# Sigmoid attention with a gated feed-forward: scores of whole key groups as three float32r products on two 64-row tiles, and six and six feed-forward tiles

## The chip, the cores and the metric

The kernel runs on one core of one Trainium2 chip. The metric is the time of one execution on the device in microseconds (us), the median of the runs shown; less is better. The profile is that of one more execution, with the hardware profiler on.

## The reference

Eight sequences of 448 tokens, 12 heads of 64 dimensions, everything in float32. Attention has a sigmoid in place of the softmax, so that no row sums are needed; its output is the input of a gated feed-forward layer of 768 to 1536 to 768.

```python
scores = scale * np.matmul(q, k.transpose(0, 1, 3, 2)) - np.log(S)
attn = 1.0 / (1.0 + np.exp(-scores))
x = np.matmul(attn, v)            # then (8*448) tokens x 768
...
gate = 1.0 / (1.0 + np.exp(-(x @ w_gate)))
val = x @ w_val
return (gate * val @ w_out).astype(np.float32)
```

The weights arrive as float64 words, which the kernel turns into a float32r part and a rest (hi and lo) by integer operations.

## The kernel before

**Attention** (lines 193 to 307). The work goes by quads of four heads: 24 quads, `m` from 0 to 23, each with the heads of two pairs, `p` 0 and 1. A quad's 448 keys of the two pairs make seven groups `g`: 0 to 2 are three groups of 128 keys of pair 0, 4 to 6 those of pair 1, and group 3 holds the last 64 keys of both pairs. One group is one beat, 168 beats in all. In each beat `scores` makes four products (the 128 keys in two halves `u`, the two heads of the pair in two halves of the partitions `h`), each 64 rows by 64 columns of the array with 448 queries streaming. The operands are float32, and TensorE runs every such product as two instructions, so that a line of four products is eight matmuls. Then comes one sigmoid on ScalarE (L221), and, two beats later (`LAG`), `values`: again four products of 64 by 64, in float32, which add up in four PSUM banks `av`.

**Beside it**, in the same loop: every second beat or so, VectorE does half of a conversion of a piece of weights (`Words.first`, L99 to L102, and `Words.second` with `finish_lo`, L112 to L118; GpSimd casts the hi part, L141). The first `J1` of twelve feed-forward tiles are converted here, 12 half steps a tile, spread over the first 156 beats (`BESIDE`). When a pair of heads is done, ScalarE copies one accumulator (L245), VectorE adds the other (L252), and the result goes to DRAM. `load_qk(m + 1)` is issued at the end of beat `g == 1`, `load_v(m + 1)` at `g == 3`. All DMAs go through SyncE's queue in the order of the program, and each engine works strictly in the order in which the loop is written.

**Feed-forward** (lines 310 to 387). For each of seven token tiles, `ff_in` makes gate and value of each feed-forward tile `j`, 36 matmuls of 128 by 128 by 512 in float32r (each product as lo·hi, hi·lo and hi·hi), and `ff_out` contracts with `w_out`, three products a tile likewise. Part one does this for the tiles `0..J1-1`, writes partial sums to DRAM and converts the other tiles (`late`) on VectorE beside it (`convert_ahead`, two half steps a call of `ff_in`); part two does the late tiles and adds the partial sums.

Of the kernel before, what the change touches and what calls it, by code (L numbers as in the profile page):

```python
# [9 lines left out]
F32R = mybir.dt.float32r  # L10
# [3 lines left out]
ALU = mybir.AluOpType  # L14
# [3 lines left out]
P = 128  # L18
HP = P // 2

F64_ZERO = 2.0 ** -15

J1 = 7

TB = 512

# [8 lines left out]
def sigmoid_attention_glu_kernel(ctx: ExitStack, tc: tile.TileContext, qk, v, wg, wv, wo, out):  # L35
# [10 lines left out]
    nc = tc.nc  # L46
    B, NQ = qk.shape[0], qk.shape[1]
    D = v.shape[-1]
    T = out.shape[-1]
    S = T // B  # L50
# [5 lines left out]
    scale = 1.0 / math.sqrt(D)  # L56
    late = list(range(J1, NJ))

# [17 lines left out]
    def chunks(j, t):  # L76
        w = (wg, wv, wo)[t]
        return [w[j][:, c * CW:(c + 1) * CW] for c in range(2)]
# [52 lines left out]
    def convert_tiles(words, js):  # L131

        for j in js:
            gv, wt = gv_tile(j, j), wo_tile(j, j)
            for to in (gv[:, 0], gv[:, 1], wt):
                for c in range(2):
                    cs = slice(c * CW, (c + 1) * CW)
                    words.first()
                    yield
                    hi, a, e = words.second()  # L140
                    nc.gpsimd.tensor_copy(to[:, 0, cs], hi)  # L141
                    finish_lo(to[:, 1, cs], a, e)
                    yield
# [27 lines left out]
    def load_x(t):  # L171
        for c in range(KT):
            xr[c] = xpool.tile([P, TB], F32, tag=f"xr{c}", name="xr")
            nc.sync.dma_start(out=xr[c], in_=x_dram[t][c])

    def split_x(cs=range(KT), cast=nc.scalar.copy):
        for c in cs:
            xh[c] = xpool.tile([P, TB], F32R, tag=f"xh{c}", name="xh")
            xl[c] = xpool.tile([P, TB], F32R, tag=f"xl{c}", name="xl")
            cast(xh[c], xr[c])  # L180
            nc.vector.tensor_tensor(out=xl[c], in0=xr[c], in1=xh[c], op=ALU.subtract)  # L181

    def store_x(b, c, x):

        at = b * S
        while at < (b + 1) * S:
            t, o = divmod(at, TB)
            n = min(TB - o, (b + 1) * S - at)
            nc.sync.dma_start(out=x_dram[t][c][:, o:o + n], in_=x[:, at - b * S:at - b * S + n])
            at += n  # L190


    halves = (slice(0, HP), slice(HP, P))
    with tc.manual_schedule(), tc.tile_pool(name="att", bufs=2) as att, tc.tile_pool(name="sc", bufs=2, space=PSUM) as scp, \
            tc.tile_pool(name="av", bufs=1, space=PSUM) as avp:
        loads, avs, pending, adds, stores = {}, {}, [], [], []

        def load_qk(m):

            if m < B * NQ:  # L200
                loads[m] = [att.tile([P, 2, 2 * S], F32, tag="qk", name="qk")]
                nc.sync.dma_start(out=loads[m][0], in_=qk[m // NQ, m % NQ])

        def load_v(m):
            if m < B * NQ:
                loads[m].append(att.tile([P, 7, 2, D], F32, tag="v", name="v"))
                nc.sync.dma_start(out=loads[m][1], in_=v[m // NQ, m % NQ])

        def scores(m, g):


            qkt = loads[m][0]
            sc = scp.tile([P, 2, 512], F32, tag="sc", name="sc")
            for h in range(2):
                for u in range(2):
                    p = u if g == 3 else g // 4
                    k0 = S + (3 * P if g == 3 else g % 4 * P + u * HP)
                    nc.tensor.matmul(sc[halves[u], h, :S], lhsT=qkt[halves[h], p, k0:k0 + HP], rhs=qkt[halves[h], p, :S],  # L218
                                     start=True, stop=True)
            a = att.tile([P, 2, S], F32, tag="a", name="a", bufs=3)  # L220
            nc.scalar.activation(a, sc[:, :, :S], AF.Sigmoid, bias=bias, scale=scale)  # L221
            return a

        def values(m, g, a):

            vt = loads[m][1]
            for u in range(2):
                p = u if g == 3 else g // 4
                key = (2 * m + p, u)
                start = key not in avs  # L230
                if start:
                    avs[key] = avp.tile([P, 512], F32, tag=f"av{p}{u}", name="av")
                last = (3 if u == 0 else 2) if p == 0 else 6
                for h in range(2):
                    nc.tensor.matmul(avs[key][halves[h], :S], lhsT=vt[halves[u], g, h], rhs=a[halves[u], h],  # L235
                                     start=start, stop=g == last)
            if g == 3:
                finish(2 * m)
            if g == 6:
                finish(2 * m + 1)  # L240

        def finish(n):
            b, c = divmod(n, 2 * NQ)
            x = att.tile([P, S], F32, tag="x", name="x")
            nc.scalar.copy(x, avs.pop((n, 0))[:, :S])  # L245
            adds.append((x, avs.pop((n, 1))[:, :S]))
            stores.append((beat + 2, b, c, x))

        def finish_adds():
            while adds:  # L250
                x, other = adds.pop()
                nc.vector.tensor_tensor(out=x, in0=other, in1=x, op=ALU.add)  # L252

        def finish_stores():
            while stores and stores[0][0] <= beat:
                store_x(*stores.pop(0)[1:])

        def load_first():

            loads[0] = [att.tile([P, 2, 2 * S], F32, tag="qk", name="qk")]  # L260
            for p, cs in ((0, slice(0, S + P)), (0, slice(S + P, 2 * S))):
                nc.sync.dma_start(out=loads[0][0][:, p, cs], in_=qk[0, 0][:, p, cs])
            load_v(0)
            nc.sync.dma_start(out=loads[0][0][:, 1], in_=qk[0, 0][:, 1])

        def warm_up(n):

            for _ in range(n):
                sc = scp.tile([P, 2, 512], F32, tag="sc", name="sc")
                for h in range(2):  # L270
                    for u in range(2):
                        nc.tensor.matmul(sc[halves[u], h, :S], lhsT=zeros[halves[h], :HP], rhs=zeros[halves[h], :S],  # L272
                                         start=True, stop=True)

        load_first()
        warm_up(2)
        words = Words(att, [c for j in range(J1) for t in (0, 1, 2) for c in chunks(j, t)], AHEAD)
        weights, n_weights, done = convert_tiles(words, range(J1)), 2 * 6 * J1, 0

        first_x = 2 * NQ + 2  # L280
        beat = 0
        for m in range(B * NQ):
            for g in range(7):
                pending.append((m, g, scores(m, g)))
                if len(pending) > LAG:
                    values(*pending.pop(0))
                finish_stores()
                if g == 1:
                    load_qk(m + 1)
                if g == LAG + 1:  # L290
                    load_v(m + 1)
                beat += 1
                while done < n_weights and done * BESIDE < beat * n_weights:
                    next(weights)
                    done += 1
                finish_adds()
                if m == first_x and g == 0:
                    load_x(0)
                if m == first_x + 1 and g < KT:
                    split_x([g], nc.gpsimd.tensor_copy)  # L300
        while pending:
            values(*pending.pop(0))
            finish_adds()
        beat += 2
        finish_stores()
        for _ in weights:
            pass


    with tc.manual_schedule(), tc.tile_pool(name="ff", bufs=2, reuse_waits="tile") as ff, \  # L310
# [52 lines left out]
        for part_two in (False, True):  # L363
            js = late if part_two else list(range(J1))
            for t in range(NT):
# [58 lines left out]
```

## Time and profile before

| | us |
|---|---|
| median of 3 runs | 1293.71 |
| lowest and highest | 1293.63, 1294.17 |
| the profiled execution, its own time | 1294.82 |
| its span, first to last instruction | 1292.7 |

The span is the time between the first and the last instruction that the profiler shows; about 2.1 us lie around it. The profiled execution was 1.1 us longer than the median.

A profile is read here by these views: the page's summary (busy time of each engine, the clock that TensorE was granted), the chain of work that ended last, the groups of instructions by line (count, busy time, mean length of one in ns, idle time before them), the timeline (start, length, engine, line, and in brackets the idle time before and what ended it), and windows (busy time of every engine in a stretch, with the number of instructions). PE is TensorE's matmul, PEld its weight load, DVE is VectorE, ACT ScalarE, POOL GpSimd, SP SyncE. The length of a matmul in the profile includes the way through the array, so that lengths overlap; the pace is read from the starts.

### The profile page before, as it was taken

To read this page: it belongs to the slowest core of one execution; us is meant where nothing else is said; L and a number is where in the kernel's file an instruction comes from. 1 tells how busy PE (TensorE), PEld (TensorE's weight loads), DVE (VectorE), ACT (ScalarE), POOL (GpSimd) and SP (SyncE) were. 2 spreads that over 40 slices of the span, in tenths; PEclk is the share of its full clock that TensorE was granted. 3 is DMA by queue.
4 is the path that set the end of the run, shared out by engine and by line. 5 is a ranking of instruction groups with operands and counts; after the bars stand their busy time and mean duration, and the time that the engine had idled before them with its cause. 6 is when DMAs were issued, how large, how long until landed. Compare 5 with 4: busy or idle time off the path is not lost.

```text
span 1292.7 us, 17701 instructions
## 1 busy us (share of the span) xinstructions
PE 1286.5 (100%) x7240; PEld 975.5 (75%) x7240; DVE 464.5 (36%) x920; ACT 358.5 (28%) x505; POOL 37.4 (3%) x52
## 2 busy tenths in 40 slices
PE   9999999999999999999999999999999999999998
PEld 4444444488888888888888888888888888888887
DVE  6778776445155252461310111202231213131312
ACT  6777777712112112121121121212020201111110
POOL 1112111000000000000000000000000000000000
PEclk9999999999999999999999999999999999999999
DMA  7777777343332332432002015241404131212202
GB/s 284 248 252 268 258 244 238 130 142 98 116 98 86 110 98 78 133 99 106 25 25 74 1 42 203 106 166 63 147 2 146 33 115 49 98 66 82 74 25 81
DMA packets 70784, 152.14 MB, mean 118 GB/s; under 512 B 9392, under 2 KB 26416, under 8 KB 70704
## 3 DMA queue, kind: packets, MB, share of 16 engines
q1 hardware_dynamic: 70704, 151.03, 34.6%
q8 instruction: 56, 0.92, 0.3%
q14 instruction: 24, 0.20, 0.0%
HBM read 106.17 MB, written 44.83 MB: 117 GB/s over the span
## 4 chain that ended last, share of the span: by engine, by line
PE 99%; DMA 1%; DVE 0%; issue 0%
PE acc L321 53%; PE acc L339 27%; PE sc L218 10%; PE av L235 10%; DMA qk<-qk 1%; PE sc L272 0%; DVE ob L358 0%; DVE zeros L67 0%; DVE bias L65 0%
## 5 line engine op out<-in xcount | busy, mean ns | idle before, releaser
L321 PE MATMUL acc<-xh,gv 128*128 128x512 f32 x2016 | 623.2, 389 | 0.0
L321 PEld LDWEIGHTS acc<-xh,gv 128*128 128x128 f32 x2016 | 378.6, 188 | 79.0 <-issue 0.7
L321 PE MATMUL acc<-xl,gv 128*128 128x512 f32 x1008 | 392.4, 389 | 0.0
L339 PE MATMUL acc<-hh,wo 128*128 128x512 f32 x1008 | 312.7, 389 | 0.0
L325 DVE TENSOR_TENSOR g<-acc,g 128x512 f32<-128x512 f32 x84 | 58.1, 692 | 598.4 <-PE acc L321 598.4
L321 PEld LDWEIGHTS acc<-xl,gv 128*128 128x128 f32 x1008 | 189.3, 188 | 39.2
L339 PEld LDWEIGHTS acc<-hh,wo 128*128 128x128 f32 x1008 | 189.3, 188 | 39.2
L339 PE MATMUL acc<-hl,wo 128*128 128x512 f32 x504 | 196.2, 389 | 0.0
L221 ACT ACTIVATE a<-sc,bias 128x896 f32<-128x896 f32 x168 | 169.3, 1008 | 67.8 <-PE sc L218 64.3
L218 PE MATMUL sc<-qk 64*64 64x448 f32 x1344 | 164.2, 541 | 0.6 <-DMA qk<-qk 0.6
L235 PE MATMUL av<-a,v 64*64 64x448 f32 x1344 | 163.2, 536 | 0.0
L328 ACT CAST hh<-g 128x512 fp32r<-128x512 f32 x84 | 52.1, 621 | 355.2 <-DVE g L325 355.2
L324 ACT ACTIVATE g<-acc 128x512 f32<-128x512 f32 x84 | 50.2, 598 | 338.1 <-PE acc L321 338.1
L218 PEld LDWEIGHTS sc<-qk 64*64 64x64 f32 x1344 | 61.6, 134 | 67.8 <-issue 53.8
L235 PEld LDWEIGHTS av<-a,v 64*64 64x64 f32 x1344 | 61.8, 133 | 65.3 <-issue 63.3
L339 PEld LDWEIGHTS acc<-hl,wo 128*128 128x128 f32 x504 | 94.6, 188 | 19.6
L329 DVE TENSOR_TENSOR hl<-g,hh 128x512 fp32r<-128x512 f32 x84 | 58.2, 693 | 57.7 <-ACT hh L328 57.7
L344 ACT COPY ob<-acc 128x512 f32<-128x512 f32 x42 | 24.7, 588 | 147.8 <-PE acc L339 147.8
L358 DVE TENSOR_TENSOR ob<-acc,pb 128x512 f32<-128x512 f32 x42 | 29.0, 690 | 82.5 <-PE acc L339 79.7
L252 DVE TENSOR_TENSOR x<-av,x 128x448 f32<-128x448 f32 x48 | 30.0, 624 | 64.3 <-ACT x L245 62.8
L181 DVE TENSOR_TENSOR xl<-xr,xh 128x512 fp32r<-128x512 f32 x84 | 52.4, 689 | 0.0
L180 ACT CAST xh<-xr 128x512 fp32r<-128x512 f32 x78 | 41.9, 616 | 0.0
(23 smaller groups left out, 331.2 us busy)
## 6 DMA issues: line engine op xcount, KB each, us to landing
xr<-xd SPq DMA_DIRECT2D x84, 256.0 KB, 4.4
qk<-qk SPq DMA_DIRECT2D x23, 896.0 KB, 5.2
v<-vv SPq DMA_DIRECT2D x24, 448.0 KB, 4.6
part<-ob SPq DMA_DIRECT2D x42, 256.0 KB, 2.0
pb<-part SPq DMA_DIRECT2D x42, 256.0 KB, 2.9
y<-ob SPq DMA_DIRECT2D x42, 256.0 KB, 2.0
wraw<-wg SPq DMA_DIRECT2D x24, 384.0 KB, 4.2
wraw<-wv SPq DMA_DIRECT2D x24, 384.0 KB, 4.0
```

The source lines that it names most:

```text
L180: cast(xh[c], xr[c])
L181: nc.vector.tensor_tensor(out=xl[c], in0=xr[c], in1=xh[c], op=ALU.subtract)
L218: nc.tensor.matmul(sc[halves[u], h, :S], lhsT=qkt[halves[h], p, k0:k0 + HP], rhs=qkt[halves[h], p, :S], start=True, stop=True)
L221: nc.scalar.activation(a, sc[:, :, :S], AF.Sigmoid, bias=bias, scale=scale)
L235: nc.tensor.matmul(avs[key][halves[h], :S], lhsT=vt[halves[u], g, h], rhs=a[halves[u], h], start=start, stop=g == last)
L252: nc.vector.tensor_tensor(out=x, in0=other, in1=x, op=ALU.add)
L321: nc.tensor.matmul(acc, lhsT=a, rhs=m, start=n == 0, stop=n == len(terms) - 1)
L324: nc.scalar.activation(g, acc, AF.Sigmoid)
L325: nc.vector.tensor_tensor(out=g, in0=acc, in1=g, op=ALU.mult)
L328: nc.scalar.copy(hh, g)
L329: nc.vector.tensor_tensor(out=hl, in0=g, in1=hh, op=ALU.subtract)
L339: nc.tensor.matmul(acc, lhsT=a, rhs=m, start=n == 0, stop=n == len(terms) - 1)
```

## The change

For the groups of 128 keys (all but group 3), `scores` no longer uses four float32 products of 64 by 64. The columns of q and k of a pair are split into a float32r part (`qkh`, a GpSimd cast of 128 by 896, `split_hi`) and the rest (`qkl`, a VectorE subtraction of 128 by 896, `split_lo`). Each head's scores are then three float32r products, lo·hi, hi·lo and hi·hi, on a tile of 64 rows and 128 columns; the two heads stand on the two 64-row halves of the array and write to different PSUM banks. Group 3 and `values` stay as they were. The splits and the load are put into the loop: pair 1 of the quad at hand at `g` 0 and 1, pair 0 of the next quad at `g` 4 and 5, and `load_qk(m + 1)` a beat earlier. `J1` goes from 7 to 6.

```diff
-J1 = 7
+J1 = 6
...
             sc = scp.tile([P, 2, 512], F32, tag="sc", name="sc")
-            for h in range(2):
-                for u in range(2):
-                    p = u if g == 3 else g // 4
-                    k0 = S + (3 * P if g == 3 else g % 4 * P + u * HP)
-                    nc.tensor.matmul(sc[halves[u], h, :S], lhsT=qkt[halves[h], p, k0:k0 + HP], rhs=qkt[halves[h], p, :S],
-                                     start=True, stop=True)
+            if g == 3:
+                k0 = S + 3 * P
+                for h in range(2):
+                    for u in range(2):
+                        nc.tensor.matmul(sc[halves[u], h, :S], lhsT=qkt[halves[h], u, k0:k0 + HP],
+                                         rhs=qkt[halves[h], u, :S], start=True, stop=True)
+            else:
+                hi, lo = split[g // 4]
+                k0 = S + g % 4 * P
+                for i, (k, q) in enumerate(((lo, hi), (hi, lo), (hi, hi))):
+                    for h in range(2):
+                        nc.tensor.matmul(sc[:, h, :S], lhsT=k[halves[h], k0:k0 + P], rhs=q[halves[h], :S],
+                                         start=i == 0, stop=i == 2)
...
+        def split_hi(m, p):
+            if m < B * NQ:
+                hi = att.tile([P, 2 * S], F32R, tag=f"qkh{p}", name="qkh", bufs=1)
+                nc.gpsimd.tensor_copy(hi, loads[m][0][:, p])
+                split[p] = hi, None
+
+        def split_lo(m, p):
+            if m < B * NQ:
+                hi = split[p][0]
+                lo = att.tile([P, 2 * S], F32R, tag=f"qkl{p}", name="qkl", bufs=1)
+                nc.vector.tensor_tensor(out=lo, in0=loads[m][0][:, p], in1=hi, op=ALU.subtract)
+                split[p] = hi, lo
...
         load_first()
         warm_up(2)
+        split_hi(0, 0)
+        split_lo(0, 0)
...
                 finish_stores()
+                if g == 0:
+                    load_qk(m + 1)
+                    split_hi(m, 1)
                 if g == 1:
-                    load_qk(m + 1)
+                    split_lo(m, 1)
+                if g == 4:
+                    split_hi(m + 1, 0)
+                if g == 5:
+                    split_lo(m + 1, 0)
```

TensorE in the middle of attention, before, around the first group of a quad (`sc` are the scores' banks, `av` the accumulators, `a` the sigmoid's output, numbers are buffers; a row stands for one or more matmuls of the program, the words in brackets are the semaphores that it waits for):

```order
L218 MATMUL sc_1429<-qk_1203 64x448 [waits Activation_49]
L218 MATMUL sc_1429<-qk_1203 64x448 x3
L235 MATMUL av_1436<-a_1394,v_1238 64x448 x2
L235 MATMUL av_1413<-a_1394,v_1238 64x448 x2
L218 MATMUL sc_1441<-qk_1330 64x448 [waits DMAHW5_49,Activation_49]
L218 MATMUL sc_1441<-qk_1330 64x448 x3
```

and the same place of a quad in the changed kernel:

```order
L225 MATMUL sc_1282<-qkh_1176,qkl_1199 128x448 [waits Activation_49]
L225 MATMUL sc_1282<-qkh_1176,qkl_1199 128x448
L225 MATMUL sc_1282<-qkl_1199,qkh_1176 128x448 x2
L225 MATMUL sc_1282<-qkh_1176 128x448 x2
L255 MATMUL av_1291<-a_1249,v_1095 64x448 x2
L255 MATMUL av_1268<-a_1249,v_1095 64x448 x2
L225 MATMUL sc_1296<-qkh_1255,qkl_1273 128x448 [waits DVE_49,Activation_49]
L225 MATMUL sc_1296<-qkh_1255,qkl_1273 128x448
L225 MATMUL sc_1296<-qkl_1273,qkh_1255 128x448 x2
L225 MATMUL sc_1296<-qkh_1255 128x448 x2
```

Six matmuls with 128 columns stand where four products of 64 columns stood, between `values` of 64 columns, and the first of a pair waits for VectorE where it waited for the DMA.

VectorE at the start of the program, before:

```order
L65 MEMSET bias_66 128x1
L67 MEMSET zeros_68 128x448
L99 TENSOR_SCALAR wa_213<-wraw_196 128x384 [waits DMAHW4_49]
L100 TENSOR_SCALAR wa_213<-wa_213 128x384 [waits DVE_49]
L101 TENSOR_SCALAR wt_214<-wa_213 128x384 [waits DVE_49]
L102 TENSOR_SCALAR wa_213<-wa_213 128x384 [waits DVE_49]
```

and in the changed kernel:

```order
L65 MEMSET bias_66 128x1
L67 MEMSET zeros_68 128x448
L241 TENSOR_TENSOR qkl_201<-qk_183,qkh_199 128x896 [waits DMAHW1_49,DMAHW0_49,Pool_49]
L99 TENSOR_SCALAR wa_226<-wraw_203 128x384 [waits DMAHW4_49]
L100 TENSOR_SCALAR wa_226<-wa_226 128x384 [waits DVE_49]
L101 TENSOR_SCALAR wt_227<-wa_226 128x384 [waits DVE_49]
L102 TENSOR_SCALAR wa_226<-wa_226 128x384 [waits DVE_49]
L241 TENSOR_TENSOR qkl_241<-qk_183,qkh_222 128x896 [waits DMAHW3_49,Pool_49]
```

The subtractions of the first quad's two pairs stand between the memsets and the conversions, and each waits for a GpSimd cast.

More of the change, by code (lines that the diff above doesn't have):

```diff
@@ L195, in sigmoid_attention_glu_kernel @@
             tc.tile_pool(name="av", bufs=1, space=PSUM) as avp:
-        loads, avs, pending, adds, stores = {}, {}, [], [], []
+        loads, split, avs, pending, adds, stores = {}, {}, {}, [], [], []
         def load_qk(m):
```

## The prediction

> **What bounds the kernel now.** First the page's summary and the chain of work that ended last.
>
> ```profile
> span 1292.7 us, 17701 instructions
> ...
> PE 1286.5 (100%) x7240; PEld 975.5 (75%) x7240; DVE 464.5 (36%) x920; ACT 358.5 (28%) x505; POOL 37.4 (3%) x52
> ...
> PEclk9999999999999999999999999999999999999999
> ...
> PE 99%; DMA 1%; DVE 0%; issue 0%
> PE acc L321 53%; PE acc L339 27%; PE sc L218 10%; PE av L235 10%; DMA qk<-qk 1%; PE sc L272 0%; DVE ob L358 0%; DVE zeros L67 0%; DVE bias L65 0%
> ```
>
> TensorE is the chain from end to end, at full clock. Whatever the change does to the time, it does through TensorE's pace in attention (scores and values are each 10% of the span) or through a new wait there. So the second view is the timeline of TensorE inside attention.
>
> ```profile
> 100.71 0.96 PE L235 MATMUL av<-a,v 64*64 64x448 f32 x8
> 101.46 0.96 PE L218 MATMUL sc<-qk 64*64 64x448 f32 x8
> 102.21 0.96 PE L235 MATMUL av<-a,v 64*64 64x448 f32 x8
> 102.96 0.96 PE L218 MATMUL sc<-qk 64*64 64x448 f32 x8
> ```
>
> Scores and values alternate, with a start every 0.75 us; a beat is 1.50 us. Eight matmuls in 0.75 us are two rounds of four that run side by side, 0.375 us a round. No gap stands between the rows.
>
> **The three products.** What a float32r matmul costs is read in the feed-forward, in a window without anything else (us, busy and number on TensorE, clock, DMA).
>
> ```profile
> 262.00:1288.00 1026.00, 1026.00 (x4528) 1.00 0.26 87
> ```
>
> That is 0.2266 us a matmul of 512 columns. With 448 it is 0.198 us if all of it scales (an estimate) and at most 0.2266. If the two heads' matmuls run side by side, as the four products do now, a group is three rounds: 0.595 us against 0.75, a gain of 0.155. There are 144 such groups (six a quad, 24 quads), so 22.3 us are removed; by the upper bound of 0.2266 it would be 144 x 0.07 = 10 us.
>
> **What it adds on TensorE: two changes of tile a beat.** Before, scores and values both use 64 by 64 tiles in float32. After, TensorE goes from 64 by 64 in float32 to 64 by 128 in float32r and back in every one of these beats. The trace of before has one such place, the step from attention to the feed-forward; here the timelines of matmuls and of weight loads around it.
>
> ```profile
> 257.63 2.46 PE L235 MATMUL av<-a,v 64*64 64x448 f32 x24
> 260.03 0.50 PE L321 MATMUL acc<-xh,gv 128*128 128x512 f32 x1
> 260.36 0.40 PE L321 MATMUL acc<-xl,gv 128*128 128x512 f32 x1
> 260.60 0.63 PE L321 MATMUL acc<-xh,gv 128*128 128x512 f32 x2
> ```
>
> ```profile
> 259.02 0.30 PEld L235 LDWEIGHTS av<-a,v 64*64 64x64 f32 x8 [0.45 <-ACT a L221]
> 260.02 0.19 PEld L321 LDWEIGHTS acc<-xh,gv 128*128 128x128 f32 x1 [0.70 <-issue]
> ```
>
> The 24 values matmuls are six rounds: at 0.375 each the next matmul was due at 259.88. It starts at 260.03, 0.15 late, and the second follows 0.33 behind it where 0.227 is the pace: together **0.25 us lost at one switch**. The second view says why: the weights of the next matmul are otherwise loaded while the present one streams, but here the load starts only at 260.02, after 0.70 of idle "issue", that is with nothing that the profile shows to wait for. The array emptied first, then the weights came, and only then the stream.
>
> The way back loads 64 columns. The page's groups of weight loads give the difference.
>
> ```profile
> L321 PEld LDWEIGHTS acc<-xh,gv 128*128 128x128 f32 x2016 | 378.6, 188 | 79.0 <-issue 0.7
> ...
> L235 PEld LDWEIGHTS av<-a,v 64*64 64x64 f32 x1344 | 61.8, 133 | 65.3 <-issue 63.3
> ```
>
> That is 0.055 us less, so 0.195 for the switch back, an estimate. A round trip is 0.445 us, and 144 of them are 64.1 us. The bounds: nothing, if this kind of switch does not empty the array; 0.30 us, if the lateness of 0.15 comes each time but the weights are hidden; 0.50, if both cost as the one seen. I take 0.445 because the one row there is changes the number of columns and the type just as the new switches do. It changes the number of rows too, and that is what is open.
>
> The Trainium skill has a rule here, in "TensorEngine Tiling (Array Packing)", section "Key Properties": changing the tiling mode, not just the tile, drains TensorE, and 64 by 64 and 64 by 128 stand there as two modes. The row above agrees for one change of mode; by the rule all 288 switches drain and the sum is the one below, while if only a change in rows drained, it would be that of the first rival.
>
> **The start.** The first scores now wait for a cast and a subtraction behind the first two loads.
>
> ```profile
> 0.74 0.86 SPq L262 DMA_DIRECT2D qk<-qk  x2
> ...
> 4.46 3.83 PE L218 MATMUL sc<-qk 64*64 64x448 f32 x24
> ```
>
> ```profile
> qk<-qk SPq DMA_DIRECT2D x1, 160.0 KB, 2.8
> ```
>
> ```profile
> L181 DVE TENSOR_TENSOR xl<-xr,xh 128x512 fp32r<-128x512 f32 x84 | 52.4, 689 | 0.0
> ...
> L113 DVE SCALAR_TENSOR_TENSOR wa<-wraw,wa 128x384 uint32<-128x384 uint32 x72 | 39.7, 551 | 0.0
> ...
> L141 POOL CAST gv<-wt 128x384 fp32r<-128x384 f32 x28 | 21.6, 771 | 133.3 <-DVE wt L112 133.3
> ...
> L180 POOL CAST xh<-xr 128x512 fp32r<-128x512 f32 x6 | 5.0, 855 | 0.0
> ```
>
> Both loads are issued between 0.74 and 1.60 and land 2.8 later, about 4.0. A cast of 512 elements takes 0.855 and one of 384 0.771, so 896 take 1.11 by that slope; a subtraction likewise 0.689 and 0.551, so 1.10. First scores at 6.2 in place of 4.46: +1.8 us, between 0 (landing early, cold clock no worse) and 3.6 (twice that, with the clock warming later).
>
> **The other splits** (47 casts, 47 subtractions, 1.1 us each) lie beside TensorE: four beats are between the last use of the old `qkh` and the first of the new, 7 us at 1.79 us a beat, for 2.2 us of work. Behind the subtraction on VectorE stand the conversions and the adds (L252) for which `values` waits; that costs nothing as long as VectorE has room. Its work in attention, from a timeline of VectorE and the groups of its window:
>
> ```profile
> 226.89 0.55 DVE L112 SCALAR_TENSOR_TENSOR wt<-wraw,wt 128x384 uint32<-128x384 uint32 x1
> ...
> 230.24 0.36 DVE L102 TENSOR_SCALAR wa<-wa 128x384 uint32<-128x384 uint32 x1
> ```
>
> ```profile
> L252 DVE TENSOR_TENSOR x<-av,x 128x448 f32<-128x448 f32 x46 | 28.7, 624 | 56.8 <-ACT x L245 55.3 <-DMA qk<-qk 1.5
> L114 DVE TENSOR_SCALAR we<-wt 128x384 uint32<-128x384 uint32 x42 | 27.8, 661 | 0.0
> ...
> L102 DVE TENSOR_SCALAR wa<-wa 128x384 uint32<-128x384 uint32 x42 | 15.1, 360 | 1.5
> ...
> L181 DVE TENSOR_TENSOR xl<-xr,xh 128x512 fp32r<-128x512 f32 x6 | 4.4, 750 | 0.0
> ```
>
> A whole conversion takes 3.71 us (226.89 to 230.60). In the first 156 beats there are now 36 of them (133.6), 45 adds (27.9), 45 subtractions (49.5) and the six of L181 (4.4): 215 us. At 1.79 us a beat these 156 beats last 273 us, so there is room; at the pace without switches it is gone, see the first rival.
>
> **The load, one beat earlier**, passes a load of weights and, in quad 8, the six `xr` loads on SyncE's queue; both then come up to one `qk` transfer later.
>
> ```profile
> 99.94 0.98 PE L218 MATMUL sc<-qk 64*64 64x448 f32 x8 [0.63 <-DMA qk<-qk]
> ```
>
> ```profile
> qk<-qk SPq DMA_DIRECT2D x23, 896.0 KB, 5.2
> ```
>
> The transfer takes 5.2 us, and its first reader is now the cast at `g == 4`, about 7 us on, with three beats behind that. The wait of 0.63 seen in one place may go or stay. I take 0, bounds -1 and +1 us.
>
> **Six and six tiles.** The 4536 feed-forward matmuls stay. Six conversions (22 us on VectorE) move from attention into part one; this window shows, in that order, TensorE's matmuls, its weight loads, VectorE and ScalarE there.
>
> ```profile
> 262.00:622.00 360.00, 360.00 (x1590) 298.26 (x1589) 146.73 (x318) 63.20 (x108) 0.00 (x0) 1.00 0.32 105
> ```
>
> VectorE is idle for 213 of 360 us while TensorE never is, so it costs nothing; without that cover it would be 22 us.
>
> **The sum**, on the profiled execution: 1294.8 - 22.3 + 64.1 + 1.8 = 1338.4. It was 1.1 us above the median of the runs, so **1337**. With the bounds of this case (0.30 a round trip: 144 x 0.145 = 20.9 us; 0.50 and 0.2266 a product: 144 x 0.43 = 61.9 us) and of the start it spans 1315 to 1359.
>
> **Rivals.**
>
> *No drain: faster.* Rows stay at 64, and if that is what counts, weights keep loading ahead. It decides below 0.155 us a round trip. TensorE alone then gives 1293.7 - 22.3 + 1.8 = 1273. But 156 beats would last 213 us (22 of 1.50, 134 of 1.345), against VectorE's 215: VectorE becomes a second bound. And GpSimd's casts slow it: L114, which runs beside a cast, takes 661 ns, L102 of the same kind 360. For 48 new casts 0.3 us each is up to 14 us, so 1273 to 1287. For it: scores and values keep row halves. Against it: the one switch in the trace emptied the array. The Trainium skill, "SBUF — State Buffer", section "SBUF: two separate sides", calls what slows L114 a lock on a port pair that VectorE and GpSimd share.
>
> *Only one of the two switches drains.* 144 x (0.595 + 0.25 - 0.75) = 13.7 us: 1309.
>
> *The two row tiles take turns*, so that the change does not do what it says. Six products in a row are 1.19 us: 144 x (1.19 + 0.445 - 0.75) = 127 us, 1423. Against it: the eight matmuls in 0.75 us above, of which each streams for 0.375; for it: none of them was float32r, and none had 128 columns on 64 rows.
>
> **How the numbers follow.** The forecast has 0.62, one-sided drain 0.10, no drain 0.20, taking turns 0.08. The range leaves out the last and half of the no-drain case: 1281 to 1360. No drain gives nearly all of "faster" (0.18) and a little "same" (0.04); the rest is slower, 0.78. The bound of 0.2%, 2.6 us, is about what a measurement of this kernel can tell from no change.
>
> **What would show it.** In the profile of the changed kernel, scores of a whole group should start 1.79 us apart, with about 1.04 from the first score matmul to the next values matmul, and two idle stretches of weight loads a beat that end in "issue". A beat of 1.35 to 1.45 would refute the drain; in it VectorE would show hardly any idle time and TensorE would wait for `qkl`. A start of the second head's matmuls 0.2 us behind the first, not a few hundredths, would mean turns. First scores should start near 6.2, the feed-forward last 1032 us as now. Wrong above all if the switch costs less with the rows unchanged.

## The result, and the profile after

The changed kernel takes **1331.16 us** (median of 4 runs, 1330.18 to 1331.63) against 1293.94 of the kernel before (4 runs): ratio 1.0283, 95% interval 1.0271 to 1.0296. It is 37.2 us slower; 1337 was forecast. The profiled execution took 1330.18 us, 1.0 less than the median.

The page's summary and chain of the changed kernel, as shown of the kernel before:

```profile
span 1328.0 us, 17312 instructions
...
PE 1317.4 (99%) x6952; PEld 968.4 (73%) x6952; DVE 535.8 (40%) x968; ACT 358.1 (27%) x505; POOL 80.2 (6%) x94
...
PE acc L350 52%; PE acc L368 26%; PE av L255 11%; PE sc L225 9%; PE sc L218 1%; DVE qkl L241 0%; DVE xl L181 0%; DMA qk<-qk 0%; DVE wa L99 0%; ACT a L228 0%; POOL qkh L234 0%; DVE ob L387 0%; DVE x L272 0%; DVE we L114 0%; DVE wt L112 0%
```

TensorE is still the chain, and it looks busy: "99%" does not show the loss, because the length of a matmul in the profile covers the way through the array. The share of the scores is 10% as before (9 for the whole groups and 1 for group 3), while that of the values, which were not touched, rose from 10 to 11. One has to look at starts. The timelines of TensorE's matmuls and of its weight loads in attention:

```profile
151.83 0.98 PE L255 MATMUL av<-a,v 64*64 64x448 f32 x8
152.74 0.47 PE L225 MATMUL sc<-qkh,qkl 64*128 64x448 f32 x2
153.05 0.36 PE L225 MATMUL sc<-qkl,qkh 64*128 64x448 f32 x2
153.25 0.36 PE L225 MATMUL sc<-qkh 64*128 64x448 f32 x2
153.54 0.98 PE L255 MATMUL av<-a,v 64*64 64x448 f32 x8
```

```profile
151.82 0.21 PEld L255 LDWEIGHTS av<-a,v 64*64 64x64 f32 x8 [0.30 <-issue]
152.74 0.19 PEld L225 LDWEIGHTS sc<-qkh,qkl 64*128 64x128 f32 x2 [0.70 <-issue]
152.84 0.19 PEld L225 LDWEIGHTS sc<-qkl,qkh 64*128 64x128 f32 x2
153.05 0.19 PEld L225 LDWEIGHTS sc<-qkh 64*128 64x128 f32 x2
153.54 0.21 PEld L255 LDWEIGHTS av<-a,v 64*64 64x64 f32 x8 [0.30 <-issue]
```

The profile prints float32r as f32 in matmuls. A beat is 1.71 us (151.83 to 153.54) where it was 1.50. Inside the scores, the second and third round follow as the forecast had it, 0.20 apart. But the values, the same eight matmuls as before, now take 0.91 until the scores start, not 0.75, and the first round of scores takes 0.31, not 0.20. The weights show why: those of the first scores round, and those of the first values round, are loaded only at the moment at which their matmuls start, after 0.70 and 0.30 us of idle "issue"; those of the second and third round are loaded ahead.

The step into the feed-forward, and its pace:

```profile
295.76 0.50 PE L350 MATMUL acc<-xh,gv 128*128 128x512 f32 x1
```

```profile
298.00:1322.00 1024.00, 1024.00 (x4519) 1.00 0.28 94
```

The feed-forward starts at 295.76, not 260.03, which is 35.7 us later, and lasts 1032 us as before at 0.2266 us a matmul. The span grew by 35.3 us, so all of the loss is in attention.

And one place that was not forecast, in quad 9, by the same timeline and then the granted clock (the number behind TensorE's busy time) in three windows around it:

```profile
123.37 0.98 PE L255 MATMUL av<-a,v 64*64 64x448 f32 x8
127.65 0.74 PE L225 MATMUL sc<-qkh,qkl 64*128 64x448 f32 x2 [3.29 <-DVE qkl L241]
128.16 0.61 PE L225 MATMUL sc<-qkl,qkh 64*128 64x448 f32 x2
128.53 0.60 PE L225 MATMUL sc<-qkh 64*128 64x448 f32 x2
```

```profile
123.00:127.60 4.60, 1.35 (x14) 1.00 0.32 88
127.60:130.70 3.10, 3.05 (x14) 0.50 0.44 104
130.70:134.00 3.30, 3.30 (x32) 0.96 0.67 252
```

TensorE stood 3.29 us for a subtraction on VectorE, and then ran at half its clock for the 3.1 us of the second window and a little beyond (0.96 is the mean of the third). The two beats last 5.70 and 2.59, together 4.9 us too long.

### The profile page after: what moved, and what is told of

It is laid out like the page before. It is cut to its first block, busy times and chain, and to the rows that moved or that the text cites. A ratio compares the mean times of both kernels' runs of the same rounds, so it can differ in the third digit from the quotient of the medians.

```text
span 1328.0 us, 17312 instructions
## 1 busy us (share of the span) xinstructions
PE 1317.4 (99%) x6952; PEld 968.4 (73%) x6952; DVE 535.8 (40%) x968; ACT 358.1 (27%) x505; POOL 80.2 (6%) x94
## 4 chain that ended last, share of the span: by engine, by line
PE 98%; DVE 1%; issue 0%; DMA 0%; ACT 0%; POOL 0%; SPq 0%; DVEq 0%; POOLq 0%
PE acc L350 52%; PE acc L368 26%; PE av L255 11%; PE sc L225 9%; PE sc L218 1%; DVE qkl L241 0%; DVE xl L181 0%; DMA qk<-qk 0%; DVE wa L99 0%; ACT a L228 0%; POOL qkh L234 0%; DVE ob L387 0%; DVE x L272 0%; DVE we L114 0%; DVE wt L112 0%
## 5 line engine op out<-in xcount | busy, mean ns | idle before, releaser
L225 PEld LDWEIGHTS sc<-qkh,qkl 64*128 64x128 f32 x288 | 27.2, 185 | 107.3 <-issue 105.1
L255 PEld LDWEIGHTS av<-a,v 64*64 64x64 f32 x1344 | 37.6, 132 | 54.9 <-issue 54.6
L225 PE MATMUL sc<-qkh,qkl 64*128 64x448 f32 x288 | 68.5, 471 | 5.4 <-DVE qkl L241 4.9
L241 DVE TENSOR_TENSOR qkl<-qk,qkh 128x896 fp32r<-128x896 f32 x48 | 53.2, 1107 | 6.8 <-POOL qkh L234 6.8
L234 POOL CAST qkh<-qk 128x896 fp32r<-128x896 f32 x48 | 48.0, 1001 | 89.3 <-PE sc L225 48.3
L225 PE MATMUL sc<-qkl,qkh 64*128 64x448 f32 x288 | 53.1, 364 | 0.0
```

What stands on the lines that cost most here:

```text
L225: nc.tensor.matmul(sc[:, h, :S], lhsT=k[halves[h], k0:k0 + P], rhs=q[halves[h], :S], start=i == 0, stop=i == 2)
L234: nc.gpsimd.tensor_copy(hi, loads[m][0][:, p])
L241: nc.vector.tensor_tensor(out=lo, in0=loads[m][0][:, p], in1=hi, op=ALU.subtract)
```

## The experiments

**Which part of the switch empties the array?** Scores and values now differ in two things, the shape of the tile and the type. Two kernels change one of them each. The first keeps the type float32 and takes the tile of 64 by 128, in the kernel before:

```diff
-            for h in range(2):
-                for u in range(2):
...
-                    nc.tensor.matmul(sc[halves[u], h, :S], lhsT=qkt[halves[h], p, k0:k0 + HP], rhs=qkt[halves[h], p, :S],
+                    k0 = S + g % 4 * P
+                    nc.tensor.matmul(sc[:, h, :S], lhsT=qkt[halves[h], g // 4, k0:k0 + P], rhs=qkt[halves[h], g // 4, :S],
                                      start=True, stop=True)
```

> The kernel before with one edit: the scores of a whole group as one float32 product for each head on a tile of 64 by 128, no splits, seven tiles. Streaming time is the same as before (two rounds of 0.375 us), the type never changes, the tile shape changes twice a beat. Tile theory: 144 x 0.36 = 52 us more than before, 1346. Type theory: 1294 within 3.

Measured: 1344.36 against 1294.51, ratio 1.0383 (1.0366 to 1.0400). Its timeline and weight loads:

```profile
149.72 0.93 PE L239 MATMUL av<-a,v 64*64 64x448 f32 x8
150.58 1.02 PE L222 MATMUL sc<-qk 64*128 64x448 f32 x4
151.53 0.98 PE L239 MATMUL av<-a,v 64*64 64x448 f32 x8
152.44 1.02 PE L222 MATMUL sc<-qk 64*128 64x448 f32 x4
```

```profile
151.53 0.21 PEld L239 LDWEIGHTS av<-a,v 64*64 64x64 f32 x8 [0.65 <-issue]
152.44 0.30 PEld L222 LDWEIGHTS sc<-qk 64*128 64x128 f32 x4 [0.70 <-issue]
```

No type changes, and the switch costs all of it: 1.86 us a beat (150.58 to 152.44), 0.36 more than before for the same streaming, and weights that wait. The way into 64 by 128 again takes 0.91 from the first values matmul.

The second changes the type and keeps the tile: parts in bfloat16, each product on four tiles of 64 by 64.

```diff
-                hi = att.tile([P, 2 * S], F32R, tag=f"qkh{p}", name="qkh", bufs=1)
+                hi = att.tile([P, 2 * S], BF16, tag=f"qkh{p}", name="qkh", bufs=1)
...
-                        nc.tensor.matmul(sc[:, h, :S], lhsT=k[halves[h], k0:k0 + P], rhs=q[halves[h], :S],
-                                         start=i == 0, stop=i == 2)
+                        for u in range(2):
+                            ku = k0 + u * HP
+                            nc.tensor.matmul(sc[halves[u], h, :S], lhsT=k[halves[h], ku:ku + HP], rhs=q[halves[h], :S],
+                                             start=i == 0, stop=i == 2)
```

> The changed kernel with the parts of q and k kept in bfloat16 and each of the three products made on four tiles of 64 by 64 again, so that scores and values use one tile shape and only the type changes between them. Tile theory (the change of tile shape empties the array): no switch cost, a beat of about 1.34 us in place of 1.71 on TensorE; 144 x 0.37 = 53 us less, 1278, and up to 1295 if VectorE (215 us of work for 213 us of beats) becomes the bound. Type theory (the change from float32 to another type empties it): weight loads still start only after an idle stretch of 0.3 to 0.7 us twice a beat, 1331 within 5. The scores have fewer bits here than the reference's.

Measured: 1300.64, ratio 1.0048 (1.0033 to 1.0063), 30.5 us less than the changed kernel. TensorE's matmuls, and one row of its weight loads:

```profile
151.58 0.36 PE L228 MATMUL sc<-qkh,qkl 64*64 64x448 bf16 x4
151.77 0.36 PE L228 MATMUL sc<-qkl,qkh 64*64 64x448 bf16 x4
151.96 0.36 PE L228 MATMUL sc<-qkh 64*64 64x448 bf16 x4
152.15 0.92 PE L258 MATMUL av<-a,v 64*64 64x448 f32 x8
152.90 0.36 PE L228 MATMUL sc<-qkh,qkl 64*64 64x448 bf16 x4
```

```profile
152.53 0.12 PEld L228 LDWEIGHTS <-qkl 64*64 64x64 bf16 x4 [0.23 <-issue]
```

The beat is 1.32 us and the weights for 152.90 are loaded at 152.53. So the type theory falls and the tile theory holds, from both sides. But the time is 22 us above the 1278 of TensorE alone, and 5.6 above the upper end given. The list of waits (total in us, times, longest) and the window of its attention (TensorE, weight loads, VectorE, ScalarE, GpSimd) say where it went:

```profile
PEld L228 <- DVE qkl L244: 42.7, 29, 5.4
PE sc L228 <- DVE qkl L244: 22.2, 17, 4.7
```

```profile
9.20:245.00 235.80, 214.44 (x2944) 96.24 (x2936) 214.79 (x376) 167.37 (x195) 78.33 (x84) 0.97 0.69 234
```

Weight loads waited 42.7 us for subtractions, and VectorE was busy for 214.8 of 235.8 us. Part of the weight loads' wait lies under matmuls that still stream; TensorE's matmuls themselves waited 22.2 us, 17 times, where the same wait of the changed kernel was 4.9 us, twice. With three of these stalls came a granted clock of 0.50 for 3.4 us (one is shown in the last section), which costs up to 1.7 us a time.

**Is it the number of switches?** The changed kernel with two groups of scores, then two groups of values:

```diff
-                if len(pending) > LAG:
+                while beat % 2 and len(pending) > LAG:
                     values(*pending.pop(0))
...
-            a = att.tile([P, 2, S], F32, tag="a", name="a", bufs=3)
+            a = att.tile([P, 2, S], F32, tag="a", name="a", bufs=4)
```

> The changed kernel with two groups of scores and then two groups of values, in place of one and one: the same matmuls, 84 round trips between tile shapes in place of 144. If the switch costs 0.36 us a round trip: 60 x 0.36 = 21.5 us less, 1310. If the cost lies in the products themselves (a slow float32r product on 64 rows, or weights that can't be loaded ahead for them): 1331 within 4.

Measured: 1312.76, ratio 1.0141 (1.0126 to 1.0156), 18.4 us less than the changed kernel. The first four of the six score rounds of a pair:

```profile
154.73 0.47 PE L225 MATMUL sc<-qkh,qkl 64*128 64x448 f32 x2
155.04 0.36 PE L225 MATMUL sc<-qkl,qkh 64*128 64x448 f32 x2
155.24 0.36 PE L225 MATMUL sc<-qkh 64*128 64x448 f32 x2
155.44 0.37 PE L225 MATMUL sc<-qkh,qkl 64*128 64x448 f32 x2
```

Only the first round after a switch is long (0.31); the first round of the second group, with no switch ahead of it, follows at the pace of 0.20. The cost belongs to the switch and not to the product. Of the 3 us by which the time misses the 21.5 us less that were expected, 2 are in quad 9: this kernel waits 4.49 us there for the subtraction, not 3.29, and loses 6.8 us in two pairs of beats, by their starts, not 4.9.

**Does it matter that the feed-forward has six and six tiles?** The kernel before, with this edit alone:

```diff
-J1 = 7
+J1 = 6
```

> The kernel before with J1 = 6 alone. All theories: no change, 1294 within 2.6; more than that would mean that a part of the difference is not in attention's scores.

Measured: 1294.94, ratio 1.0004 (0.9995 to 1.0013). Nothing.

**The stall in quad 9.** The changed kernel with the casts of x there by ScalarE:

```diff
-                    split_x([g], nc.gpsimd.tensor_copy)
+                    split_x([g])
```

> The changed kernel with one edit: the six casts of x in quad 9 by ScalarE in place of GpSimd. In the changed kernel two beats there last 5.70 and 2.59 us in place of 1.71, 4.9 us too long. Theory A (the GpSimd casts of x hold up the splits behind them on GpSimd and stretch VectorE's subtractions to 1.1 to 1.8 us): most of it goes, 1327 to 1329. Theory B (VectorE alone has too much to do in that quad: six more subtractions of 0.69 us): little goes, 1330 to 1332.

Measured: 1327.68, ratio 1.0254 (1.0237 to 1.0272), 3.5 us less. One wait of TensorE is left there:

```profile
126.79 0.47 PE L225 MATMUL sc<-qkh,qkl 64*128 64x448 f32 x2 [1.43 <-DVE qkl L241]
```

Theory A explains the larger part: the wait went from 3.29 to 1.43 us, and this time the granted clock stays at 1.00. What is left may be theory B; that was not separated.

**What holds the kernel without switches?** First, the bfloat16 kernel with less conversion work beside attention:

```diff
-        weights, n_weights, done = convert_tiles(words, range(J1)), 2 * 6 * J1, 0
+        weights, n_weights, done = convert_tiles(words, range(J1 - 1)), 2 * 6 * (J1 - 1), 0
...
-        weights = convert_ahead(words)
+        weights = chain(convert_tiles(words, [J1 - 1]), convert_ahead(words))
```

> The bfloat16 kernel on 64 by 64 tiles (1300.6) with the conversion of the sixth feed-forward tile moved out of attention into the first token tile of the feed-forward: six conversions of 3.7 us less on VectorE in attention. If VectorE's load is what stretches its attention from about 230 to 257 us, about 22 us come back in attention, 1279 to 1285. If the stretching is the order of the queues alone (a split that waits for its load or its cast, with VectorE idle behind it), little comes back: 1295 to 1300.

Measured: 1295.05 (10 runs, 1291.85 to 1299.18), ratio 1.0008 (0.9995 to 1.0021): 5.6 us less, of 22 us of work that were taken from VectorE. The profile shows the shortest of these runs. Then, with the splits away from their deadline too:

```diff
-                if g == 0:
-                    load_qk(m + 1)
-                    split_hi(m, 1)
-                if g == 1:
-                    split_lo(m, 1)
-                if g == 4:
-                    split_hi(m + 1, 0)
-                if g == 5:
-                    split_lo(m + 1, 0)
+                if g == 0:
+                    load_qk(m + 2)
+                if g in (2, 4):
+                    split_hi(m + 1, g // 2 - 1)
+                if g in (3, 5):
+                    split_lo(m + 1, g // 2 - 1)
```

> The same, and beside it: the splits one quad ahead with two buffers, the load of q and k two quads ahead, group 3 in the three bfloat16 products too, the casts of x by ScalarE. No tile switch and no split near its deadline: 168 beats of 1.32 us are 222 us in place of 251 before, the start 1.8 us later: 1268. If VectorE still binds (193 us of work for 206 us of beats): up to 1280.

Measured: **1271.04**, ratio 0.9819 (0.9804 to 0.9833). And this kernel with the conversions of all six tiles in attention again:

> The kernel of 1271.0 with all six tiles converted in attention again: VectorE has the load of the bfloat16 kernel (1300.6), but the splits are made a quad ahead. If lateness of the splits made up the 25 to 30 us between 1300.6 and 1271: 1271 to 1276. If VectorE's load did: 1288 to 1295.

Measured: 1283.81, ratio 0.9916 (0.9899 to 0.9932), between the two expectations. The weight loads' wait, as above, in the kernels of 1295.05, 1271.04 and 1283.81:

```profile
PEld L229 <- DVE qkl L245: 30.8, 19, 4.6
```

```profile
PEld L221 <- DVE qkl L237: 6.6, 6, 3.1
```

```profile
PEld L221 <- DVE qkl L237: 5.1, 6, 3.1
```

Splitting a quad ahead, with the edits that came with it (the load of q and k another quad earlier, two buffers, group 3 in bfloat16, the casts of x by ScalarE), takes the weight loads' wait for `qkl` from 42.7 to 5.1 us and the time from 1300.6 to 1283.8, at the same conversions on VectorE. Taking the work off VectorE after that gives 12.8 more, where it gave 5.6 before. Both counted, and the lighter load paid more once the splits were early. How much of the 16.8 us belongs to each of the edits that came together was not tried.

Last, the longest wait of TensorE left in the kernel of 1271.04 is a late `v` in quad 9, which stands behind the six loads of x on SyncE's queue:

```profile
97.66 1.77 PE L251 MATMUL av<-a,v 64*64 64x448 f32 x8 [3.59 <-DMA v<-vv]
```

```diff
-                if m == first_x and g == 0:
-                    load_x(0)
+                if m == first_x and g < KT:
+                    load_x(0, [g])
```

> The kernel of 1271.0 with the six loads of x one a beat in place of all six at once, and the load of v a beat earlier. Two beats there last 5.16 and 2.67 us in place of 1.32 behind a v that lands late: up to 5 us less, 1266 to 1268; 1271 if another wait takes its place.

Measured: 1269.71, ratio 0.9807 (0.9792 to 0.9822). Of 5 us only 1.3 came: the long stall is gone, but by the starts the eight beats from 92.5 us are still 2.9 us too long together, in several smaller waits. This is the fastest version here, 24.8 us under the kernel before; its scores are made of 16-bit parts of q and k, not of float32r ones.

## Why the prediction was right

*The mechanism* stood in it: each beat changes the tile twice, the array empties, the weights of the first round are not loaded ahead. The two changes and the late weights show in the profile after, with the two idle stretches that end in "issue"; that the array is empty by then is read from them, as no view shows it directly. The experiments tie the cost to the tile's shape. This was the open point of the prediction, since its one row changed rows, columns and type at once: columns alone suffice. The rule of the Trainium skill that it weighed ("TensorEngine Tiling (Array Packing)", "Key Properties") holds here for 64 by 64 against 64 by 128.

*The switch* was the term that was off: 0.445 us a round trip, 64.1 us. Measured it is 0.80 + 0.91 for scores and values, less 0.61 (three rounds of 0.203) and 0.75, so 0.35 us, 50 us in all. The way into 64 by 128 was estimated at 0.25 from the switch to the feed-forward and is 0.21. The dead time from the last matmul that starts to the next weights is the same in both, 0.46 us. But there the four matmuls of a round start up to 48 ns apart, while after a switch all four start within 20 ns, so that the last one starts earlier and the array should be empty sooner. The way back, which was scaled from 0.25 by the columns of the weights, was off more: 0.14, not 0.195. That is 0.29 from the last score round to the values, where 0.20 is the pace, and 0.05 by which the first values round is longer (0.427 between the starts of its rounds, not 0.376). The last score round streams for 0.20 us where one of values takes 0.375; the idle stretch of the weight loads is shorter too, 0.30 in place of 0.70.

*The products*: 0.198 forecast, 0.20 seen; the two heads run side by side (`x2` within a few ns). The gain was 144 x 0.14 = 20 us, forecast 22.3.

*The start*: first scores at 6.2 forecast, 6.33 measured, through the cast and the subtraction:

```profile
4.12 0.93 POOL L234 CAST qkh<-qk 128x896 fp32r<-128x896 f32 x1 [3.68 <-DMA qk<-qk]
...
5.09 1.09 DVE L241 TENSOR_TENSOR qkl<-qk,qkh 128x896 fp32r<-128x896 f32 x1 [3.73 <-POOL qkh L234]
...
6.33 0.47 PE L225 MATMUL sc<-qkh,qkl 64*128 64x448 f32 x2 [1.65 <-DVE qkl L241]
```

What the forecast did not have: a little after this wait, too, TensorE's clock falls to half (granted clock behind TensorE's busy time).

```profile
8.11:11.52 3.41, 3.21 (x18) 0.50 1.05 422
```

The beat from the first values on lasts 2.42 us, where the same beat of other quads lasts 1.55. The first values start 9.73 against 8.11 in the kernel before, only 1.6 later.

*The other splits*, costed at nothing, and *the load*, at nothing with bounds of 1 us, cost 4.9 us in one quad. The step that failed is the even spread of VectorE's work: 215 us in 156 beats left room on the average, but the six subtractions of x, their casts and a split share a few beats of quad 9, and there the load's sum does not say when a split is done. The wait of 0.63 us for `qk` went, as one of the two cases said.

*Six and six tiles*: nothing, as forecast.

*The sum by these sizes*: beats 144 x 0.21 = 30, start 1.9 (first values 1.6 later and 0.9 in the beat at half clock, less the 3 x 0.21 that stand in the beats already), quad 9 4.9, less 1.4 that the kernel before lost (0.86 in the beat with the wait of 0.63 us for `qk`, and 0.57 around 118 us, where 72 matmuls take 7.32 us and not 6.75), is 35.4 of the 35.7 us by which the feed-forward starts later. The forecast had 43.6. That it came as near is in part luck: the switches were 14 us too dear, and quad 9, at nothing, and the products made up 7 of them.

*The rival without a drain* had VectorE as second bound right, but put its price at 14 us at most: 1273 to 1287. The bfloat16 kernel, which is near that case (no switch, rounds of 0.19 us), took 1300.6. A split near its deadline stalls TensorE while VectorE still has room: 22.2 us of waits with VectorE busy for 214.8 of 235.8 us, and the half clock with three of them.

## What to carry to other kernels

When a product gets cheaper on another tile shape, count how often the shape alternates with that of its neighbours: here a round trip cost 0.35 us and the cheaper product saved 0.14. Either give both neighbours one shape, or batch them, and look at whether weight loads still start ahead of their matmuls; the busy share will not tell. Work that a matmul waits for should be done well ahead, here a whole quad, before one counts on the helper engine's average load.

## What the runs showed of the hardware

In the changed kernel a stall of 3.29 us was followed by a granted clock of 0.50; with the casts of x on ScalarE one of 1.43 us in the same quad was followed by none. The length of the stall alone does not decide it. Two stalls of the bfloat16 kernel, each with the granted clock behind it:

```profile
47.96 0.38 PE L228 MATMUL sc<-qkh,qkl 64*64 64x448 bf16 x4 [1.96 <-DVE qkl L244]
...
150.24 0.38 PE L228 MATMUL sc<-qkh,qkl 64*64 64x448 bf16 x4 [1.92 <-DVE qkl L244]
```

```profile
48.68:52.10 3.42, 3.42 (x32) 0.50 0.34 85
150.24:154.00 3.76, 3.76 (x60) 1.00 0.53 105
```

The Trainium skill ("TensorE: Matmul & The Clock Gate", "Part 1: The HAM clock gate") puts the idle window after which the clock is halved at about 3.4 us. The stall of 3.29 us comes near that and the one of 1.96 us does not; what decides between 1.96 and 1.92 stays open here.

GpSimd's casts stretch VectorE's subtractions of 896 elements where they overlap: two of the changed kernel's 48 do, and take 1.49 and 1.81 us in place of 1.08. For the second of them TensorE waited in the stall above:

```profile
125.69 1.81 DVE L241 TENSOR_TENSOR qkl<-qk,qkh 128x896 fp32r<-128x896 f32 x1
...
130.01 1.08 DVE L241 TENSOR_TENSOR qkl<-qk,qkh 128x896 fp32r<-128x896 f32 x1
```
